# First query block's attention: three score buffers, values of two key tiles a visit, and queries projected with the whole array into one bank

## The chip, the cores and the metric

The kernel runs on one core of one Trainium2 chip. Its engines work from queues of their own and meet through semaphores: TensorE (PE, which multiplies and writes only the eight banks of PSUM; its weight loads are listed apart as PEld), VectorE (DVE), ScalarE (ACT), GpSimd (POOL) and SyncE (SP, which here only starts transfers). Each queue runs in order: an instruction that waits holds up all that stand behind it on its engine. The metric is the device time of one execution in microseconds (us), as the median of several runs; smaller is better.

## The reference

A transformer block on one sequence of 2048 tokens of width 576, in float32: multi-query attention with 32 query heads of 18 and one shared head of keys and values, then a bilinear feed-forward layer of inner width 4608.

```python
def _A_ref(x, wq, wk, wv, wo):
    q = (x @ wq).reshape(B, S, 32, 18).transpose(0, 2, 1, 3)
    k, v = x @ wk, x @ wv
    p = softmax(einsum("bhqd,bkd->bhqk", q, k) * 18 ** -0.5)
    o = einsum("bhqk,bkd->bhqd", p, v)
    return o.transpose(0, 2, 1, 3).reshape(B, S, 576) @ wo

def _B_ref(x, w_gate, w_up, w_down):
    return ((x @ w_gate) * (x @ w_up)) @ w_down

h = x + _A_ref(_layernorm(x), wq, wk, wv, wo)
out = h + _B_ref(_layernorm(h), w_gate, w_up, w_down)
```

## The kernel before

The queries are cut into four blocks of 512 tokens (`TB`), the keys into 16 tiles of 128, the heads into eight groups of four. Attention of one block and one group takes 32 **pairs** (`pair`): a pair multiplies one tile of keys with the queries of two heads (`scores`, L701: two matmuls, each on one half of the array's rows, side by side, into the two banks of a score buffer `s`) and lets ScalarE write the exponentials of that buffer, 128 x 1024, into a tile `P` (L702). Two pairs make the four heads of one key tile; that tile then waits in `pend` until `flush` multiplies it with the values (`values`, L706: eight instructions that work on columns of the array in groups of 32) and adds to the bank `acc`. When all 16 tiles are in, VectorE transposes `acc` into `os` (`turn`, L732) and normalises it (`normalise`, L787 to L794) a round or two later. The eight groups of one block are 256 pairs. Softmax is taken against an upper bound of each score row, which is worked out from sums of absolute queries: `bounds` (L554 on TensorE, then three VectorE operations on a tile `m2`) and `bounds_last` (L543) for the last four heads of all blocks.

Everything is put in order by hand (`manual_schedule`): the order of the calls in the Python program is the order in every queue. The stages are these.

- `keys_values` normalises x, makes keys and values and the first two sevens of block 0's queries, and has done six pairs when it ends.
- The **loop** in `run` (L1600) goes on with the attention of block 0. Beside it run, from a generator `rest`, the remaining fourteen projections of queries (`queries`, seven heads each: 14 steps over the parts of the contraction, L498), and from `down_weights` one step of the work that splits the down weights into a high and a low part (DMA loads by GpSimd, sums L1519 and casts L1527 on GpSimd, subtractions L1533 on VectorE, stores L1539 by SP). A round of the loop is: pair, some steps of a projection (2.3 a round on average, `RATE`; a finished projection counts 4), pair, `run_aux`, values of all but the newest key tile, one step of the weights' work.
- A step of a projection is two matmuls of 64 rows each, side by side on the two halves of the array's rows, into two banks `psq` and `psr` of the tag `f`. At the end VectorE adds the two and splits the sum into a high and a low part `qs` (L505 to L508), SP stores it (L510, L511), and VectorE writes its absolute values `tq` (L515). The tiles `qs`, `m2` and `m2l` share one tag with two buffers, used in turn.
- After the loop, plain rounds (`steps`) go on to the end of group 7 (pair 224), where the bounds are tested (`flag`, `guard`). Group 7's pairs follow, among output projections (L880) that use the banks `f`, and then `ffn`, block by block, with the attention of the later blocks between its matmuls.

PSUM is fully used: two score buffers `s` of two banks (four banks), two banks `f`, one `m`, one `a`. The bank of `acc` is `a` for even and `m` for odd groups of block 0 (`ps_acc`), and `bounds` takes the other one.

Of the kernel before, what the change touches and what calls it, by code (L numbers as in the profile page):

```python
# [18 lines left out]
F32 = mybir.dt.float32  # L19
# [38 lines left out]
class Block:  # L58
# [8 lines left out]


    def ps_s(self, name):
        return self.ps.tile([P, 2, TB], F32, tag="s", bufs=2, name=name)  # L70

    def ps_f(self, name):
        return self.ps.tile([P, TB], F32, tag="f", bufs=2, name=name)

    def ps_m(self, name):
        return self.ps.tile([P, TB], F32, tag="m", bufs=1, name=name)
# [10 lines left out]

    def ps_acc(self, b, g):

        self.in_m = b == 0 and g < 6 and g % 2 == 1  # L90
        return (self.ps_m if self.in_m else self.ps_a)(f"acc{b}_{g}")


    def split(self, hi, lo, src, copy=None):
# [44 lines left out]
    def keys_values(self):  # L139

        pe, act, dve, sp, pool = self.pe, self.act, self.dve, self.sp, self.nc.gpsimd
# [33 lines left out]
        rs, xhs, trs, psks, tq_last = {}, {}, [], {}, []  # L175
# [196 lines left out]
        _, _, tail = trs.pop()  # L372
# [38 lines left out]
        psg = []  # L411
# [43 lines left out]
        psg = bound(kab, self.ps_m("psb1"))  # L455
# [17 lines left out]
    def queries(self, b):  # L473

        pe, act, dve, sp = self.pe, self.act, self.dve, self.sp
        for i, (h0, n) in enumerate(QT):
            r = n * DH
            psq = self.ps_f(f"psq{b}_{i}")
            w_h, w_l = self.wq[i]
            if b == 0 and i < 2:  # L480
                for k, (w, m) in enumerate(passes(w_h, w_l, self.XT[b])):
                    pe.matmul(psq[:r], w, m, start=(k == 0), stop=(k == 13))
                    yield 1
                qs = self.qb.tile([P, 2, TB], F32R, tag="qs", name=f"qs{b}_{i}")
                act.copy(qs[:r, 0], psq[:r])
                if i == 0:
                    yield 0
                    t = f32(self.qb.tile([P, 2, TB], F32R, tag="qs", name="q_f")[:r, 0])
                    act.copy(t, psq[:r])
                    self.nc.gpsimd.tensor_tensor(qs[:r, 1], t, f32(qs[:r, 0]), ALU.subtract)  # L490
                else:
                    dve.tensor_tensor(qs[:r, 1], psq[:r], f32(qs[:r, 0]), ALU.subtract)
            else:

                psr = self.ps_f(f"psr{b}_{i}")
                for k, (w, m) in enumerate(passes(w_h, w_l, self.XT[b])):
                    for o, ps in ((0, psq), (64, psr)):
                        pe.matmul(ps[:r], w[o:o + 64], m[o:o + 64], start=(k == 0), stop=(k == 13))  # L498
# [6 lines left out]
                dve.tensor_copy(t, psr[:r])  # L505
                dve.tensor_tensor(f32(qs[:r, 1]), psq[:r], t, ALU.add)
                dve.tensor_copy(qs[:r, 0], f32(qs[:r, 1]))
                dve.tensor_tensor(qs[:r, 1], f32(qs[:r, 1]), f32(qs[:r, 0]), ALU.subtract)  # L508
            rows = self.q_dram[b, h0 * DH:h0 * DH + r]
            sp.dma_start(rows[:, 0:2, :], f32(qs[:r]))  # L510
            sp.dma_start(rows[:, 2, :], f32(qs[:r, 0]))  # L511
# [6 lines left out]
        if b == NB - 1:  # L518
            yield 4
            self.bounds(b)  # L520

    def bounds(self, b, copy=None, m2=None, psg=None):

        pe, dve, sp = self.pe, self.dve, self.sp
        if psg is None:
            psg = (self.ps_a if self.in_m else self.ps_m)(f"psg{b}_{self.known[b]}")
# [136 lines left out]

    def p_tile(self, shape, name):

        i = self.p_next = (self.p_next + 1) % (P_BUFS + (P2_BUFS if self.p2 is not None else 0))
        pool, tag = (self.pp, "P") if i < P_BUFS else (self.p2, "P2")
        return pool.tile(shape, F32, tag=tag, name=name)

    def more(self, b):  # L670
# [20 lines left out]

    def again_scores(self, n):

        to = [self.ps_f(f"again{i}") for i in range(2)]
        for _ in range(n):
            for i, o in enumerate((0, 64)):
                self.pe.matmul(to[i], self.kT[o:o + 56, 0:P], self.q[o:o + 56, 0], start=True, stop=True)

    def scores(self, s_, p_, q, t, pr):
        for i, o in enumerate((0, 64)):  # L700
# [855 lines left out]
    def run(self):  # L1556
        from contextlib import ExitStack
        tc = self.tc
# [13 lines left out]
        self.tqs, self.in_m = [], False  # L1572
        self.p2, self.p_next, self.wo_from, self.due = None, -1, 10 ** 6, 0.0
        with ExitStack() as st:
            pool = lambda name, bufs, **k: st.enter_context(tc.tile_pool(name=name, bufs=bufs, **k))
            cp, self.lp, self.hp = pool("const", 1), pool("ln", 2), pool("resid", 2)
# [8 lines left out]
            with tc.tile_pool(name="p0q", bufs=1) as self.p0q:  # L1585
                self.wq_in, self.wq = self.wq, {}
                self.XT = [self.p0q.tile([P, 9, TB], F32R, tag=f"XT{b}", name=f"XT{b}") for b in range(NB)]
                self.G = self.p0q.tile([P, 64], F32R, name="G")
                with tc.tile_pool(name="qb", bufs=2) as self.qb:
                    first = self.keys_values()  # L1590
# [230 lines left out]
```

## Time and profile before

| | us |
|---|---|
| median of 3 runs (lowest, highest) | 2250.22 (2249.98, 2252.01) |
| the profiled execution | 2249.05 |
| its span, first to last instruction | 2247.3 |
| TensorE busy in the span | 2222.8 (99%) |
| ScalarE busy | 1434.3 (64%) |
| VectorE busy | 1373.1 (61%) |
| GpSimd busy | 902.6 (40%) |

A line of the profile names an engine, a line of the kernel, an operation, its tiles (out<-in), a count, and microseconds. In a timeline the first number is the start from the beginning of the span, the second how long the group of like instructions lasted; what stands in brackets is idle time of that engine just before, and what ended it. Matmuls overlap, so that the time a matmul takes from the queue is read from start to start, not from its own length.

### The profile page before, as it was taken

Reading aid. Unit: us, or ns where it says so; the run is one execution under the profiler, and the core shown is the slowest. Engines: PE = TensorE matmul, PEld = TensorE weight load, DVE = VectorE, ACT = ScalarE, POOL = GpSimd, SP = SyncE. Lnnn points to the kernel's source line nnn. Section 1 sums busy time; section 2 is a strip of 40 time slices with the busy share of each in tenths; the row PEclk is TensorE's granted clock in tenths of the full one; section 3 lists DMA queues with packets and bytes.
Section 4 is the critical chain, followed back from the end, with each engine's and each line's share of the span. In section 5 each row is a group of like instructions: output and inputs, shape, how many; then the busy total and the mean of one; then the engine's idle time right before and its main releaser. Section 6 shows DMA issues by size and latency. Waiting matters only on the chain.

```text
span 2247.3 us, 45977 instructions
## 1 busy us (share of the span) xinstructions
PE 2222.8 (99%) x17972; PEld 1626.0 (72%) x17972; DVE 1373.1 (61%) x2206; ACT 1434.3 (64%) x1948; POOL 902.6 (40%) x979
## 2 busy tenths in 40 slices
PE   7999999999999999999999999999999999999999
PEld 5333345777777777777777777777777888999999
DVE  8565635565556557455555556545555668888776
ACT  7888877656666666666665666665666534555553
POOL 4444401444344435344444434433332465322222
PEclk9999999999999999999999999999999999999999
DMA  5878843555455565555455554664332445677775
GB/s 176 274 252 291 296 152 96 165 172 169 153 169 166 164 187 160 172 171 175 152 167 163 180 160 160 179 196 148 116 121 96 145 150 200 221 238 239 235 247 174
DMA packets 200625, 407.01 MB, mean 181 GB/s; under 512 B 22573, under 2 KB 54445, under 8 KB 200405
## 3 DMA queue, kind: packets, MB, share of 16 engines
q1 hardware_dynamic: 197813, 393.42, 54.2%
q0 software_dynamic: 2592, 10.62, 1.5%
q8 instruction: 143, 2.34, 0.4%
q14 instruction: 77, 0.63, 0.1%
HBM read 317.27 MB, written 74.55 MB: 174 GB/s over the span
## 4 chain that ended last, share of the span: by engine, by line
PE 83%; DVE 1%; DMA 1%; POOL 1%; ACT 1%; issue 0%; SPq 0%; ACTq 0%; DVEq 0%; POOLq 0%
PE pg L1104 21%; PE acc L706 15%; PE y L1044 13%; PE s L701 9%; PE gs L1330 8%; PE pu L1104 5%; PE yq L1296 4%; PE gu L1104 3%; PE yo L880 3%; PE gs L1337 2%; PE y L1011 1%; DMA h<-in_x_dram 1%; POOL h L1054 0%; PE tx L934 0%; DMA out_dram<-h 0%
## 5 line engine op out<-in xcount | busy, mean ns | idle before, releaser
L702 ACT ACTIVATE P<-s 128x1024 f32<-128x1024 f32 x1024 | 1009.4, 1028 | 214.4 <-PE s L701 131.8
L1104 PE MATMUL pg<-X,ws 64*128 64x512 f32 x2511 | 679.6, 389 | 0.5 <-DVE os L732 0.2
L1104 PE MATMUL pu<-X,ws 64*128 64x512 f32 x2511 | 679.8, 389 | 0.0
L1104 PEld LDWEIGHTS pg<-X,ws 64*128 64x128 f32 x2511 | 465.0, 185 | 77.3 <-issue 2.1
L706 PE MATMUL acc<-P,V 128*32 128x512 f32 x4096 | 479.5, 597 | 0.1
L1104 PEld LDWEIGHTS pu<-X,ws 64*128 64x128 f32 x2511 | 464.5, 185 | 13.5
L701 PE MATMUL s<-q,kT 56*128 56x512 f32 x2048 | 421.3, 414 | 4.8 <-ACT P L702 4.0
L1054 POOL TENSOR_TENSOR h<-h,tmp 128x288 f32<-128x288 f32 x320 | 259.8, 843 | 321.9 <-ACT tmp L1053 320.5
L1053 ACT COPY tmp<-y 128x288 f32<-128x288 f32 x320 | 127.8, 400 | 336.5 <-PE y L1044 307.3
L1044 PEld LDWEIGHTS y<-wdo,room 128*128 128x128 f32 x2142 | 289.7, 188 | 42.4 <-issue 37.7
L701 PEld LDWEIGHTS s<-q,kT 56*128 56x128 f32 x2048 | 194.4, 184 | 172.6 <-ACT P L702 122.7
L1044 PE MATMUL y<-wdo,room 128*128 128x288 f32 x2142 | 303.5, 300 | 1.1 <-DVE room L97 1.0
L706 PEld LDWEIGHTS acc<-P,V 128*32 128x32 f32 x4096 | 114.4, 109 | 254.5 <-issue 250.1
L1050 DVE TENSOR_TENSOR h<-h,y 128x288 f32<-128x288 f32 x394 | 169.5, 453 | 182.5 <-PE y L1044 179.4
L969 DVE TENSOR_TENSOR ws<-wr,ws 128x1152 fp32r<-128x1152 f32 x108 | 189.4, 1754 | 107.3 <-POOL ws L966 107.3
L1142 DVE TENSOR_TENSOR hf<-pu,hf 128x512 f32<-128x512 f32 x93 | 63.8, 686 | 221.5 <-ACT hf L1138 221.5
L966 POOL CAST ws<-wr 128x1152 fp32r<-128x1152 f32 x108 | 131.7, 1220 | 143.0 <-DMA wr<-in_wgu_dram 131.4
L96 POOL CAST room<-hf 128x256 fp32r<-128x256 f32 (+1 forms) x92 | 58.1, 632 | 315.5 <-DVE hf L1142 315.5
L1279 POOL TENSOR_TENSOR wsum<-wsum,wsum 128x512 f32<-128x512 f32 x72 | 145.9, 2026 | 46.4 <-DMA wsum<-in_wgs_dram 39.3
L97 DVE TENSOR_TENSOR room<-hf,room 128x256 fp32r<-128x256 f32 (+1 forms) x108 | 95.4, 883 | 3.4 <-ACT room L96 1.8
L1104 PE MATMUL gu<-X,ws 64*128 64x512 f32 x810 | 94.6, 389 | 0.0
L1104 PEld LDWEIGHTS gu<-X,ws 64*128 64x128 f32 x810 | 78.6, 184 | 13.6 <-issue 1.3
(268 smaller groups left out, 2760.2 us busy)
## 6 DMA issues: line engine op xcount, KB each, us to landing
wdo<-wd_dram SPq DMA_DIRECT2D x492, 288.0 KB
wr<-in_wgu_dram SPq DMA_DIRECT2D x108, 576.0 KB
wsum<-in_wgs_dram SPq DMA_DIRECT2D x108, 256.0 KB
wd_dram<-wd_room SPq DMA_DIRECT2D x20, 1008.0 KB
wsum_dram<-wsum SPq DMA_DIRECT2D x72, 256.0 KB
raw<-wsum_dram SPq DMA_DIRECT2D x72, 256.0 KB
q<-q_dram SPq DMA_DIRECT2D x64, 216.0 KB
raw<-in_wgs_dram SPq DMA_DIRECT2D x54, 256.0 KB
```

The source lines that it names most:

```text
L701: self.pe.matmul(s_[:, i], self.kT[o:o + 56, t * P:(t + 1) * P], q[o:o + 56, pr], start=True, stop=True)
L702: self.act.activation(p_, s_, AF.Exp, scale=SCALE)
L706: self.pe.matmul(acc[32 * j:32 * j + 32, :], self.V[:, t, :], Ps[j // 2][:, j % 2, :], start=first, stop=last, skip_group_check=True)
L966: self.nc.gpsimd.tensor_copy(w[:, 0], self.wr[n])
L969: self.dve.tensor_tensor(w[:, 1], self.wr.pop(n), f32(w[:, 0]), ALU.subtract)
L1044: pe.matmul(y[:, :HD], m[:, t * P:(t + 1) * P], k, start=(first and j == 0), stop=(j == 2), skip_group_check=True)
L1050: dve.tensor_tensor(hs, hs, y[:, :HD], ALU.add)
L1053: act.copy(z, y[:, :HD])
L1054: pool.tensor_tensor(hs, hs, z, ALU.add)
L1104: pe.matmul(ps, w[o:o + 64, wk, c], X[o:o + 64, xk, c], start=(j == 0), stop=(j == 26))
L1279: pool.tensor_tensor(to, x, y, op)
L1330: pe.matmul(bank[:, g * HT:(g + 1) * HT], W[:, wk, c, g], X[:, 2 * xk + c], start=(first and g == c == wk == xk == 0), stop=(c == 1 and wk ...
```

## The change

1. While the two banks `f` aren't needed (from the end of `keys_values` to eight pairs after the guard), they are a third score buffer `s3`, and every third pair uses it. After that the pool `f` is opened again.
2. A new loop, `trio`, takes the place of the old one. A round has four pairs and two steps of the weights' work, and the values of two key tiles in one visit: pair, a run of a projection's steps, pair, pair, pair, values of two tiles.
3. A step of a projection is one matmul over all 128 rows of the array into one bank, `m`. The runs are written out: 5, 5, 4 steps in three rounds for twelve of the projections, 4, 4, 3, 3 for the last two. VectorE makes high and low part with two operations instead of four.
4. `bounds` and `bounds_last` wait in a list `late` and get a round of their own, in place of a run, at the end of a projection. They use the bank `m` too, and `acc` always uses `a`.
5. The exponentials' tiles `P` get four more buffers (`P1`) during the loop. `again_scores`, which keeps TensorE at work at the guard, takes a score buffer instead of two banks `f`.

The diff, without what only renames or makes room:

```diff
     def ps_s(self, name):
+        self.n_s += 1
+        if self.pf is None and self.n_s % 3 == 0:
+            return self.p3.tile([P, 2, TB], F32, tag="s3", bufs=1, name=name)
         return self.ps.tile([P, 2, TB], F32, tag="s", bufs=2, name=name)
...
     def ps_acc(self, b, g):
-        self.in_m = b == 0 and g < 6 and g % 2 == 1
-        return (self.ps_m if self.in_m else self.ps_a)(f"acc{b}_{g}")
+        return self.ps_a(f"acc{b}_{g}")
...
-        self.aux.append((self.round + 1, lambda: self.bounds_last(tq_last), None))
+        self.late.append(lambda: self.bounds_last(tq_last))
...
     def queries(self, b):
...
-                psr = self.ps_f(f"psr{b}_{i}")
+                psq = self.ps_m(f"psq{b}_{i}")
                 for k, (w, m) in enumerate(passes(w_h, w_l, self.XT[b])):
-                    for o, ps in ((0, psq), (64, psr)):
-                        pe.matmul(ps[:r], w[o:o + 64], m[o:o + 64], start=(k == 0), stop=(k == 13))
+                    pe.matmul(psq[:r], w, m, start=(k == 0), stop=(k == 13))
                     if k < 13:
                         yield 1
-                    if self.tqs and self.tqs[0][0] < max(b, 1) and (b and k == 12 or k >= 5 and 4 <= self.n_pair % (2 * NT) < 2 * NT - 6):
-                        self.bounds(self.tqs[0][0])
                 qs = self.qb.tile([P, 2, TB], F32R, tag="qs", name=f"qs{b}_{i}")
-                t = f32(qs[:r, 0])
-                dve.tensor_copy(t, psr[:r])
-                dve.tensor_tensor(f32(qs[:r, 1]), psq[:r], t, ALU.add)
-                dve.tensor_copy(qs[:r, 0], f32(qs[:r, 1]))
-                dve.tensor_tensor(qs[:r, 1], f32(qs[:r, 1]), f32(qs[:r, 0]), ALU.subtract)
+                dve.tensor_copy(qs[:r, 0], psq[:r])
+                dve.tensor_tensor(qs[:r, 1], psq[:r], f32(qs[:r, 0]), ALU.subtract)
...
             self.tqs.append((b, h0, n, tq))
+            if i == 3 or b == 0 and i:
+                self.late.append(lambda: self.bounds(b))
...
+    def trio(self, others, work):
+        self.pair()
+        runs, z = iter(RUNS), 4
+        while z or self.late:
+            self.pair()
+            if self.late and z != 1:
+                self.late.pop(0)()
+            else:
+                for _ in range(next(runs, 1)):
+                    z = next(others, None)
+            self.run_aux(1)
+            next(work, None)
+            self.pair()
+            self.pair()
+            self.pair()
+            self.flush(2)
+            self.run_aux(1)
+            next(work, None)
+        self.pair()
...
     def run(self):
...
                     first = self.keys_values()
+                    two.close()
+                    self.pf = None
+                    self.p3 = two.enter_context(tc.tile_pool(name="s3", bufs=1, space=PSUM))
...
-                    others, live, due = rest(), True, 0.0
-                    while live:
-                        self.pair()
-                        due += RATE
-                        while due > 0 and live:
-                            z = next(others, None)
-                            live = z is not None
-                            due -= z or 0
-                        self.pair()
-                        self.run_aux(1)
-                        self.flush(len(self.pend) - 1)
-                        next(work, None)
+                    with tc.tile_pool(name="P1", bufs=P1_BUFS) as self.p1:
+                        self.trio(rest(), work)
...
             self.steps(lambda: self.n_pair < n + 8)
+            two.close()
+            self.p3, self.pf = None, pool("f", 1, space=PSUM)
...
-RATE = 2.3
+RUNS = (5, 5, 4) * 12 + (4, 4, 3, 3) * 2
+P1_BUFS = 4
```

More of the change, by code (lines that the diff above doesn't have):

```diff
@@ L69, in ps_s @@
     def ps_s(self, name):
+        self.n_s += 1
+        if self.pf is None and self.n_s % 3 == 0:
+            return self.p3.tile([P, 2, TB], F32, tag="s3", bufs=1, name=name)
         return self.ps.tile([P, 2, TB], F32, tag="s", bufs=2, name=name)
     def ps_f(self, name):
-        return self.ps.tile([P, TB], F32, tag="f", bufs=2, name=name)
+        return self.pf.tile([P, TB], F32, tag="f", bufs=2, name=name)
     def ps_m(self, name):
@@ L477, in queries @@
             r = n * DH
-            psq = self.ps_f(f"psq{b}_{i}")
             w_h, w_l = self.wq[i]
             if b == 0 and i < 2:
+                psq = self.ps_f(f"psq{b}_{i}")
                 for k, (w, m) in enumerate(passes(w_h, w_l, self.XT[b])):
@@ L493, in queries @@
             else:
-                psr = self.ps_f(f"psr{b}_{i}")
+                psq = self.ps_m(f"psq{b}_{i}")
                 for k, (w, m) in enumerate(passes(w_h, w_l, self.XT[b])):
-                    for o, ps in ((0, psq), (64, psr)):
-                        pe.matmul(ps[:r], w[o:o + 64], m[o:o + 64], start=(k == 0), stop=(k == 13))
+                    pe.matmul(psq[:r], w, m, start=(k == 0), stop=(k == 13))
                     if k < 13:
                         yield 1
-                    if self.tqs and self.tqs[0][0] < max(b, 1) and (b and k == 12 or k >= 5 and 4 <= self.n_pair % (2 * NT) < 2 * NT - 6):
-                        self.bounds(self.tqs[0][0])
                 qs = self.qb.tile([P, 2, TB], F32R, tag="qs", name=f"qs{b}_{i}")
-                t = f32(qs[:r, 0])
[L505 to L508, printed above, removed]
+                dve.tensor_copy(qs[:r, 0], psq[:r])
+                dve.tensor_tensor(qs[:r, 1], psq[:r], f32(qs[:r, 0]), ALU.subtract)
+                del psq
             rows = self.q_dram[b, h0 * DH:h0 * DH + r]
@@ L516, in queries @@
             self.tqs.append((b, h0, n, tq))
+            if i == 3 or b == 0 and i:
+                self.late.append(lambda: self.bounds(b))
             yield 0 if b == 0 and i < 2 else 4
-        if b == NB - 1:
-            yield 4
-            self.bounds(b)
     def bounds(self, b, copy=None, m2=None, psg=None):
@@ L525, in bounds @@
         if psg is None:
-            psg = (self.ps_a if self.in_m else self.ps_m)(f"psg{b}_{self.known[b]}")
+            psg = self.ps_m(f"psg{b}_{self.known[b]}")
         self.bound_rows(psg, self.tqs)
@@ L664, in p_tile @@
     def p_tile(self, shape, name):
-        i = self.p_next = (self.p_next + 1) % (P_BUFS + (P2_BUFS if self.p2 is not None else 0))
-        pool, tag = (self.pp, "P") if i < P_BUFS else (self.p2, "P2")
+        i = self.p_next = (self.p_next + 1) % (P_BUFS + (P2_BUFS if self.p2 is not None else P1_BUFS if self.p1 is not None else 0))
+        pool, tag = (self.pp, "P") if i < P_BUFS else (self.p1, "P1") if self.p2 is None else (self.p2, "P2")
         return pool.tile(shape, F32, tag=tag, name=name)
@@ L692, in again_scores @@
     def again_scores(self, n):
-        to = [self.ps_f(f"again{i}") for i in range(2)]
+        to = self.ps_s("again")
         for _ in range(n):
             for i, o in enumerate((0, 64)):
-                self.pe.matmul(to[i], self.kT[o:o + 56, 0:P], self.q[o:o + 56, 0], start=True, stop=True)
+                self.pe.matmul(to[:, i], self.kT[o:o + 56, 0:P], self.q[o:o + 56, 0], start=True, stop=True)
     def scores(self, s_, p_, q, t, pr):
@@ L1571, in run @@
         self.n_pair, self.half, self.pend, self.aux, self.round, self.on, self.saving = 0, [], [], [], 0, True, None
-        self.tqs, self.in_m = [], False
-        self.p2, self.p_next, self.wo_from, self.due = None, -1, 10 ** 6, 0.0
+        self.tqs, self.late = [], []
+        self.pf = self.p1 = self.p2 = self.p3 = None
+        self.n_s = 0
+        self.p_next, self.wo_from, self.due = -1, 10 ** 6, 0.0
         with ExitStack() as st:
@@ L1589, in run @@
                 with tc.tile_pool(name="qb", bufs=2) as self.qb:
+                    two = ExitStack()
+                    self.pf = two.enter_context(tc.tile_pool(name="f", bufs=1, space=PSUM))
                     first = self.keys_values()
+                    two.close()
+                    self.pf = None
+                    self.p3 = two.enter_context(tc.tile_pool(name="s3", bufs=1, space=PSUM))
                     work = self.down_weights()
@@ L1598, in run @@
                     self.cast = self.dve.tensor_copy
[L1599 to L1610 removed]
+                    with tc.tile_pool(name="P1", bufs=P1_BUFS) as self.p1:
+                        self.trio(rest(), work)
+                    self.p1 = None
             assert self.n_mx <= 8
```

## The prediction

> **What bounds the kernel now.** I read first the chain of work that ended last, then the loop's stretch alone, from exponential to exponential, then who waits for whom in it, and last TensorE's starts one by one.
>
> ```profile
> PE 83%; DVE 1%; DMA 1%; POOL 1%; ACT 1%; issue 0%; SPq 0%; ACTq 0%; DVEq 0%; POOLq 0%
> ```
>
> TensorE carries the whole span, so what it gains in the first attention ends earlier, if later work isn't held by something else. The loop, by engines (PE, PEld, DVE, ACT, POOL busy, each with its count, then the granted clock, the DMA share and GB/s), and two waits inside it:
>
> ```profile
> 52.69:276.90 224.21, 223.34 (x1632) 85.31 (x1629) 131.17 (x154) 197.77 (x205) 107.73 (x123) 1.00 0.82 275
> ```
>
> ```profile
> ACT P L702 <- PE s L701: 26.4, 89, 1.2
> ...
> PE s L701 <- ACT P L702: 0.8, 4, 0.3
> ```
>
> One of the 205 exponentials began before the stretch and the next after it begins at 277.01 (below), so 204 pairs take 224.3 us, 1.10 each, or 4.40 for four. ScalarE is short of work 89 times (26.4 us); TensorE's matmuls waited for a score buffer 4 times, 0.8 us together. So it is TensorE's own queue that sets the pace. Two rounds of it:
>
> ```profile
> 124.42 1.06 PE L706 MATMUL acc<-P,V 128*32 128x512 f32 x8
> 125.42 0.50 PE L701 MATMUL s<-q,kT 56*128 56x512 f32 x2
> 125.76 0.40 PE L498 MATMUL psq<-XT,wq 64*126 64x512 f32 x1
> ...
> 126.00 0.39 PE L498 MATMUL psq<-XT,wq 64*126 64x512 f32 x1
> ...
> 126.47 0.40 PE L701 MATMUL s<-q,kT 56*128 56x512 f32 x2
> 126.79 1.07 PE L706 MATMUL acc<-P,V 128*32 128x512 f32 x8
> ...
> 128.93 1.07 PE L706 MATMUL acc<-P,V 128*32 128x512 f32 x8
> ```
>
> From start to start: the values of one tile 1.00, the scores behind them 0.34, a step of a projection 0.23 or 0.24 (three of them from 125.76 to 126.47), scores ahead of the values 0.32. A round with three steps is 2.37, with two 2.14. Scores in mid-stream cost 0.23 too (the next fence), so that 0.11 of the 0.34 and 0.09 of the 0.32 are the change between rows in halves and columns in quarters, and the values lose 0.09 at their end.
>
> **The change, part by part.** First a round of `trio` on TensorE, from these starts:
>
> ```profile
> 44.79 1.88 PE L482 MATMUL psq<-XT,wq 128*126 128x512 f32 x7
> 46.60 0.64 PE L706 MATMUL acc<-P,V 128*32 128x512 f32 x4
> ...
> 282.31 0.49 PE L701 MATMUL s<-q,kT 56*128 56x512 f32 x2
> 282.74 1.11 PE L554 MATMUL psg<-tq,G 126*32 126x512 f32 x4
> 283.78 0.50 PE L701 MATMUL s<-q,kT 56*128 56x512 f32 x2
> ...
> 285.20 0.75 PE L701 MATMUL s<-q,kT 56*128 56x512 f32 x4
> 285.88 1.07 PE L706 MATMUL acc<-P,V 128*32 128x512 f32 x8
> ...
> 293.45 1.80 PE L697 MATMUL again<-q,kT 56*128 56x512 f32 x14
> ...
> 428.91 4.05 PE L706 MATMUL acc<-P,V 128*32 128x512 f32 x36
> 432.89 0.67 PE L1044 MATMUL y<-wdo,room 128*128 128x288 f32 x3
> ```
>
> - Values of two tiles: 36 instructions take 3.98 (428.91 to 432.89); less one tile's 1.00, 28 take 2.98, or 0.85 for eight. Two tiles in a visit: 1.85 instead of 2.00.
> - Scores between values and a run: 0.43 (282.31 to 282.74), for they change mode on both sides.
> - A run of five whole-array steps between other modes: seven take 1.81 (44.79 to 46.60), less two at 0.23: 1.35. A step costs no more and no less than one of two halves.
> - Three scores behind the run: two between other modes 0.68 (285.20 to 285.88), the one in the middle 0.23 (six spacings of the seven like pairs at 293.45, (1.80 - 0.40) / 6): 0.91, or 0.89 by the 0.34 and 0.32 above. I take 0.89.
>
> A round with five steps is 1.85 + 0.43 + 1.35 + 0.89 = 4.52, with four 4.29, with three 4.06. The old loop does five steps and four pairs in 2.37 + 2.14 = 4.51. What the double visit saves, the change to the whole array and back eats: a round has four changes of mode, as two old ones had. `RUNS` gives 24 rounds of five, 16 of four, 4 of three; there are seven `late` rounds, four with four bound matmuls (1.04, 282.74 to 283.78; round 4.21) and three with one (3.5 on TensorE, but four exponentials need 3.7, and buffers must come free: 3.8).
>
> The page TensorEngine Tiling of the Trainium skill (Key Properties) says that a change of tiling mode, not of tile, drains the array, which speaks against the runs; the rows agree with about 0.2 a change. Were the whole array free of it, the sum would be that of the second rival below.
>
> **The third buffer** lets TensorE score three pairs in a row. An exponential follows the one before by 0.92 (four in 3.77, the last 1.02 long):
>
> ```profile
> 277.01 3.82 ACT L702 ACTIVATE P<-s 128x1024 f32<-128x1024 f32 x4 [0.20 <-PE s L701]
> ...
> 285.80 3.77 ACT L702 ACTIVATE P<-s 128x1024 f32<-128x1024 f32 x4 [0.39 <-PE s L701]
> ...
> 289.92 1.94 ACT L702 ACTIVATE P<-s 128x1024 f32<-128x1024 f32 x2 [0.35 <-PE s L701]
> ...
> 293.46 1.94 ACT L702 ACTIVATE P<-s 128x1024 f32<-128x1024 f32 x2 [1.60 <-PE s L701]
> ...
> 296.20 3.77 ACT L702 ACTIVATE P<-s 128x1024 f32<-128x1024 f32 x4 [0.80 <-PE s L701]
> 300.21 1.94 ACT L702 ACTIVATE P<-s 128x1024 f32<-128x1024 f32 x2 [0.24 <-ACT P L702]
> ```
>
> Four need 3.7 of a round's 4.5: no wait on TensorE in full rounds, nor a gain there beyond the rounds' own sum. With two buffers only, three scores in a row would wait. The ten `P` tiles cover up to seven live ones.
>
> **The wait at the start.** `m2`, `m2l` and `qs` take turns in two buffers. The old order gave `m2l` a free one and `m2` that of the second projection, still being stored:
>
> ```profile
> 57.31 0.68 DVE L97 TENSOR_TENSOR m2l<-psgl,m2l 32x512 fp32r<-32x512 f32 x1
> ...
> 64.72 0.68 DVE L96 CAST m<-psg 32x512 fp32r<-32x512 f32 x1 [6.14 <-DMA q_dram<-qs]
> 65.44 0.68 DVE L97 TENSOR_TENSOR m<-psg,m 32x512 fp32r<-32x512 f32 x1
> ```
>
> ```profile
> 60.22 0.43 SPq L510 DMA_DIRECT2D q_dram<-qs  x1
> 60.70 0.38 SPq L511 DMA_DIRECT2D q_dram<-qs  x1
> ```
>
> VectorE stood 6.14 us, and TensorE went on, for the bound lay in a bank that it didn't need. In `trio` the first late round takes `m2`, the second `m2l`, and it is `m2l` that gets the buffer under store. SP's queue ahead of that store is as before, so the split of `psgl` again begins at 64.72 and ends at 66.1. But `psgl` is now in bank `m`, and so is the projection that comes in the third round. TensorE would be there at about 61.1 (52.7, where the stretch's first exponential begins, two late rounds of 3.8 and 4.2, 0.43) and stands until 66.1: 5 us, of which nothing comes back, as ScalarE isn't the bound. Behind it stand all scores and values.
>
> **The sum.** From 66.1: the rest of that round 4.09, then 23 x 4.52 + 16 x 4.29 + 4 x 4.06 + 2 x 3.8 + 3 x 4.21 = 209.1, so pair 211 is scored at 279.3. Its exponential begins 0.6 later (285.20 to 285.80). Twelve more by the third buffer, at 0.93, bring pair 223's to 291.1, and as before the last values and pair 224's scores follow, 2.62 after it (290.84, which is 289.92 and 0.92, to 293.46): 293.7 against 293.46. So the loop is some 2 later, and the plain rounds (1.03 a pair before, and the last bounds now inside the loop) give it back. The eight pairs after the guard save 8 x (1.00 - 0.93) = 0.6 (1.00 from 296.20 to 300.21). Together -0.4.
>
> **Other edits.** VectorE per projection, with the two that remain at 0.69 each:
>
> ```profile
> L506 DVE TENSOR_TENSOR qs<-psq,qs 126x512 f32<-126x512 f32 x14 | 9.7, 692 | 0.5
> ...
> L505 DVE COPY qs<-psr 126x512 f32<-126x512 f32 x14 | 9.6, 685 | 27.4 <-PE psr L498 27.3
> ...
> L507 DVE CAST qs<-qs 126x512 fp32r<-126x512 f32 x14 | 8.1, 577 | 0.5
> L508 DVE TENSOR_TENSOR qs<-qs 126x512 fp32r<-126x512 f32 x13 | 12.1, 929 | 0.5
> ```
>
> 2.88 become 1.38: 21 us less of an engine that isn't the bound, worth nothing by itself. The bank is read by both, so it is free 1.4 after the last step. After a run of four the last step ends 1.6 into its round and the bank is wanted at 4.29 + 0.43: slack 1.7. `acc` in one bank must be transposed between two visits:
>
> ```profile
> L732 DVE STREAM_TRANSPOSE os<-acc x7: 703/709/717, 85.7 to 293.0; 128x512 f32<-128x512 f32 x7
> ```
>
> 0.71, with 4.52 - 1.85 = 2.7 between the visits: slack 2.0, six times. Both are hidden as long as VectorE is no later than that. It has waits in the loop that can make it so:
>
> ```profile
> DVE wd_room L1533 <- POOL wd_room L1527: 24.0, 6, 6.2
> DVE wd_src L1533 <- POOL wd_hi L1527: 12.4, 4, 4.8
> ```
>
> Ends: 0 if each falls where VectorE has nothing to hand over, some 10 if five of these ten waits (3.6 on average) stand ahead of a bank's last reader and exceed the slack by 2.0. The weights' work keeps its pace, one step for two pairs, and subtractions mostly stand behind the readers in the order of the calls; I take 0.7. The loads of group 1's queries move a little in SP's queue, behind the same store; they are wanted some twenty pairs later, so nothing. `again_scores` in the third buffer and the reopened `f` (first used by projections a dozen pairs on): nothing, their cover being the exponential two pairs back. Transfers: the same bytes.
>
> So -0.4 + 0.7 = 0.3. The profiled execution (2249.05, of which 1.75 lies around the span) would become 2249.3; the median stands 1.17 above it, which makes 2250.5.
>
> **The rivals.** A measurement of this kernel can tell about 0.2%, 4.5 us, from no change.
>
> 1. No wait at the start: the store lands before 61, or `m2l` gets another buffer. Then 5 us less, 2245.5. For it: only one wait of before shows the late landing. Against: SP issues that store behind the same transfers.
> 2. The change of mode doesn't show around the runs, weights being loaded ahead: a run then costs 5 x 0.23, the scores around it 0.32 and 0.23, in all 0.4 less a round, 44 times: 17 us, 2233. Against: the seven steps at 44.79 take 0.2 more than 7 x 0.23, and the scores at 282.31 the longer 0.43.
> 3. The buffers were the bound, and ScalarE's 26.4 us come back: 2224. Perfetto Trace Analysis of the Trainium skill (Optimization Strategy) reads regular gaps on the engine that should be saturated as possibly too few buffers in PSUM. But the gaps are ScalarE's, and the 0.8 us on TensorE bounds what buffers can give in full rounds.
> 4. Slower: VectorE, held by GpSimd's casts, hands bank `m` or `acc` over late, and TensorE stands, which two spare banks hid before. Decisive from 4 us of such waits in all; with five of ten, as above, 2259.
>
> **How the numbers follow.** My forecast, no change, 0.55; the first rival 0.16; second and third together 0.08; the fourth 0.21. Of the first, half ends beyond 4.5 us. The forecast's own range is 2247 to 2254 (40 full rounds known to 0.05 each, and 0 to 4 for VectorE). All told 2243 to 2258 leaves out the second and third and part of the fourth. Faster 0.18, the same 0.62, slower 0.20.
>
> **What would show it.** Rounds of five at 4.5 with a run of 1.35 and values of 1.85; VectorE's `m2l` waiting for `q_dram` until about 64.7 and TensorE's first `psq` of the loop at 66.1; pair 224's exponential at 293 to 294. Wrong, if the rounds are shorter than 4.4, if that `psq` starts before 63, or if TensorE waits for VectorE at the banks for more than 4 us.

## The result: 0.5% slower, by two long waits of TensorE and the clock after them

| | before | after |
|---|---|---|
| median, us (lowest, highest) | 2250.1 (2249.78, 2252.01) | 2262.59 (2262.21, 2264.65) |
| profiled execution, us | 2249.05 | 2264.65 |
| its span, us | 2247.3 | 2262.9 |
| ratio of the times | | 1.0054, interval 1.0042 to 1.0067 |

In the experiments below, one execution of two (5605.59) and one of plain3 (3615.15) were slow, and no time or ratio given here includes them.

The change costs 12.5 us, outside the range that was given (2243 to 2258). Following single pairs through both traces shows where. The exponential of pair 210 begins 14.9 us later than before, that of pair 224 (where the prediction put 293.7) 13.3 later, that of pair 260 12.6 later; 1.5 is added between pairs 276 and 285, and from pair 300 to the last pair the distance stays at 14.1 to 14.7. So nearly all of it arises in the loop, between 51 and 280 us. ScalarE's timeline of after, at pair 224:

```profile
306.76 1.94 ACT L698 ACTIVATE P<-s 128x1024 f32<-128x1024 f32 x2 [1.66 <-PE s L697]
```

The rounds themselves have the sizes that were predicted. A full round of five steps on TensorE's timeline of after:

```profile
133.08 1.92 PE L702 MATMUL acc<-P,V 128*32 128x512 f32 x16
134.93 0.50 PE L697 MATMUL s<-q,kT 56*128 56x512 f32 x2
135.36 1.43 PE L499 MATMUL psq<-XT,wq 128*126 128x512 f32 x5
136.72 0.96 PE L697 MATMUL s<-q,kT 56*128 56x512 f32 x6
137.61 1.92 PE L702 MATMUL acc<-P,V 128*32 128x512 f32 x16
```

From start to start, values 1.85, scores 0.43, five steps 1.36, three scores 0.89: 4.53. Over the loop the median of the 24 rounds of five is 4.53, of the 16 rounds of four 4.30, of the four rounds of three 4.07 (predicted 4.52, 4.29, 4.06). What is new are two rounds of 11.68 and 10.95 us, and three of 5.26 to 5.48. The waits of TensorE from 51 to 290 us in after (tile and line that waited, what ended it; total, times, longest), without the 0.8 us in all that it waited for score buffers:

```profile
PE psq L499 <- DVE m2l L99: 5.3, 1, 5.3
PE psg L550 <- DVE qs L504: 5.2, 1, 5.2
PE psq L499 <- DVE qs L504: 1.1, 1, 1.1
```

The first is the wait that the prediction had at 5.0. Its place in TensorE's timeline, and the two rows of VectorE that end it:

```profile
61.14 0.50 PE L697 MATMUL s<-q,kT 56*128 56x512 f32 x2
66.98 2.47 PE L499 MATMUL psq<-XT,wq 128*126 128x512 f32 x5 [5.35 <-DVE m2l L99]
69.38 1.65 PE L697 MATMUL s<-q,kT 56*128 56x512 f32 x6
70.96 2.64 PE L702 MATMUL acc<-P,V 128*32 128x512 f32 x16
73.53 0.50 PE L697 MATMUL s<-q,kT 56*128 56x512 f32 x2
```

```profile
65.44 0.68 DVE L98 CAST m2l<-psgl 32x512 fp32r<-32x512 f32 x1 [9.73 <-DMA q_dram<-qs]
66.16 0.68 DVE L99 TENSOR_TENSOR m2l<-psgl,m2l 32x512 fp32r<-32x512 f32 x1
```

`m2l` waits for the store of `qs`, as foreseen. But look at what follows: five steps take 2.40 from start to start where a round at rest has 1.36, three scores 1.58 instead of 0.89, values 2.57 instead of 1.85. The windows around both waits say why. The columns after the busy times (with counts) of PE, PEld, DVE, ACT and POOL are the granted clock, the DMA share and GB/s:

```profile
61.70:65.60 3.90, 0.00 (x0) 0.00 (x0) 0.16 (x1) 1.06 (x2) 3.70 (x5) 1.00 0.77 241
65.70:66.90 1.20, 0.00 (x0) 0.00 (x0) 1.17 (x3) 0.00 (x0) 0.00 (x0) 0.50 0.70 154
66.98:72.40 5.42, 5.42 (x19) 2.69 (x23) 2.68 (x3) 2.16 (x3) 1.58 (x3) 0.50 0.90 315
72.60:77.00 4.40, 4.40 (x33) 1.90 (x29) 0.00 (x0) 2.60 (x4) 3.27 (x4) 1.00 0.71 250
...
157.70:161.10 3.40, 0.00 (x0) 0.00 (x0) 2.94 (x2) 1.02 (x2) 2.03 (x3) 1.00 0.19 47
161.30:162.70 1.40, 0.00 (x0) 0.00 (x0) 1.37 (x4) 0.00 (x0) 0.00 (x0) 0.50 0.66 249
162.77:168.00 5.23, 5.23 (x22) 1.85 (x26) 2.50 (x4) 2.46 (x3) 3.92 (x6) 0.50 0.83 276
```

Some 4 us after TensorE's last matmul the clock goes to half here; it comes back 6.83 us later (72.5 and 168.0), though TensorE is at work again from 66.98 and 162.77. The rest of the round after the first wait lasts 6.55 us (66.98 to 73.53) instead of 4.09: 2.5 us on top of the wait. The second stretch covers 5.23 us of work at half speed, by estimate some 2.6. Before, the clock stands at 1.00 through the whole loop. The Trainium skill, TensorE: Matmul & The Clock Gate (Part 1: The HAM clock gate), has the clock halved after an idle window of some 3.4 us. These two stretches agree, with 4.0 and 3.6 us from the last matmul; other runs below do not (store: 2.0 us after the last matmul; fill and shift: after waits of 2.4 and 1.6 us), and there the measurement decides.

The second wait is a chain over four engines. Its rows on SP, GpSimd, VectorE and TensorE, one timeline each:

```profile
129.57 0.31 SPq L507 DMA_DIRECT2D q_dram<-qs  x1
...
132.66 3.10 SPq L799 DMA_DIRECT2D ob<-ob  x4
135.87 0.58 SPq L1556 DMA_DIRECT2D wd_dram<-wd_hi  x1
136.54 0.61 SPq L1556 DMA_DIRECT2D wd_dram<-wd_src  x1
```

```profile
145.64 0.57 POOL L1530 DMA_DIRECT2D wd_src<-in_wd_dram  x1 [11.16 <-DMA wd_dram<-wd_src]
154.09 3.19 POOL L1536 TENSOR_TENSOR wd_src<-wd_src 128x288 f32<-128x288 f32 x4 [7.87 <-DMA wd_src<-in_wd_dram]
157.22 1.99 POOL L1544 CAST wd_hi<-wd_src 128x864 fp32r<-128x864 f32 x2
```

```profile
126.90 1.32 DVE L1550 TENSOR_TENSOR wd_src<-wd_src,wd_hi 128x1152 f32<-128x1152 f32 x1
...
158.16 3.23 DVE L1550 TENSOR_TENSOR wd_src<-wd_src,wd_hi 128x864 f32<-128x864 f32 x2 [13.96 <-POOL wd_hi L1544]
161.31 0.68 DVE L503 CAST qs<-psq 126x512 fp32r<-126x512 f32 x1
162.02 0.69 DVE L504 TENSOR_TENSOR qs<-psq,qs 126x512 fp32r<-126x512 f32 x1
```

```profile
157.09 0.50 PE L697 MATMUL s<-q,kT 56*128 56x512 f32 x2
162.77 1.91 PE L550 MATMUL psg<-tq,G 126*32 126x512 f32 x4 [5.18 <-DVE qs L504]
```

VectorE had finished the piece of the down weights at 128.2, but its store stands one step of the weights' work later in the program, in SP's queue behind the stores of the queries and of `ob` (which waits for `normalise`). It is issued at 136.5 and has landed at 145.6; only then may GpSimd load the next piece into that tile. Sums and casts follow, and VectorE waits 13.96 us for the cast. Behind that subtraction stand L503 and L504, the only readers of bank `m`, and TensorE needs the bank for `psg`. Reading a wait to its end pays here: the table names `qs`, the cause is a store some 25 us before, as the run store below bears out.

### The profile page after: what moved, and what is told of

Read it like the earlier page. It is cut to its first block, busy times and chain, and to the rows that moved or that the text cites. A ratio compares the mean times of both kernels' runs of the same rounds, so it can differ in the third digit from the quotient of the medians.

```text
span 2262.9 us, 45557 instructions
## 1 busy us (share of the span) xinstructions
PE 2225.7 (98%) x17776; PEld 1635.1 (72%) x17776; DVE 1350.3 (60%) x2181; ACT 1428.2 (63%) x1948; POOL 900.7 (40%) x979
## 4 chain that ended last, share of the span: by engine, by line
PE 89%; DVE 3%; DMA 3%; ACT 1%; POOL 1%; issue 1%; SPq 0%; ACTq 0%; POOLq 0%; DVEq 0%
PE pg L1100 19%; PE acc L702 18%; PE y L1040 13%; PE s L697 11%; PE gs L1326 8%; PE pu L1100 6%; PE yq L1292 4%; PE gu L1100 3%; PE yo L876 3%; PE psq L499 2%; PE gs L1333 2%; DMA wd_dram<-wd_room 1%; ACT P L698 1%; PE y L1007 1%; POOL h L1050 0%
## 5 line engine op out<-in xcount | busy, mean ns | idle before, releaser
L702 PE MATMUL acc<-P,V 128*32 128x512 f32 x4096 | 471.0, 597 | 0.1
L697 PE MATMUL s<-q,kT 56*128 56x512 f32 x2048 | 404.1, 413 | 4.5 <-ACT P L698 3.5
L702 PEld LDWEIGHTS acc<-P,V 128*32 128x32 f32 x4096 | 120.8, 110 | 271.6 <-issue 265.1
```

The costliest lines, as they stand in the source:

```text
L697: self.pe.matmul(s_[:, i], self.kT[o:o + 56, t * P:(t + 1) * P], q[o:o + 56, pr], start=True, stop=True)
L702: self.pe.matmul(acc[32 * j:32 * j + 32, :], self.V[:, t, :], Ps[j // 2][:, j % 2, :], start=first, stop=last, skip_group_check=True)
```

## The experiments

The first theory: the two long waits, each with its stretch of half clock, make the 13 us, and the parts of the round cost what was predicted. Its rivals: the half clock is no consequence of the waits (then shortening TensorE's idle time saves the wait alone); VectorE is late everywhere, so that moving one wait brings up another; and, for the parts that the prediction costed at nothing, that the whole array or the third buffer costs something else than the round's sum.

**The first wait alone (own).** `m2l` in a buffer of its own, one `P1` buffer less for room:

```diff
-        m2 = self.qb.tile([H, 2, TB], F32R, tag="qs", name="m2l")
+        m2 = self.qb.tile([H, 2, TB], F32R, tag="m2l", bufs=1, name="m2l")
-P1_BUFS = 4
+P1_BUFS = 3
```

> m2l has a buffer of its own (for room, three more exponentials' tiles P instead of four). Theory 1, that each of TensorE's two long waits costs its length and then some 2.7 us at half clock: the wait of 5.3 us before the loop's first whole-array step goes, and with it the first stretch at half clock, 8.1 us less than the changed kernel, about 2254.5; the second wait, near 157, stays. Theory 2, that the waits only show a loop held back by the weights' work and its transfers: the time moves to later waits, no less than 2260.

Measured: 2256.76, ratio to the kernel before 1.0032 (1.0020 to 1.0044); 5.8 less than after, where 8.1 were expected. In the profiled execution, the fastest of six (2255.34), the wait and its half clock are gone; at pair 64 the kernel is 1.0 ahead of before where after is 6.7 behind. Pair 224 is 4.0 late. What is left is the second wait, 4.0 us, with a stretch of 3.4 us at half clock. The other executions show lower mean clocks (down to 0.997), and no trace shows where. The long wait, and the window:

```profile
PE psg L550 <- DVE qs L504: 4.0, 1, 4.0
```

```profile
154.70:158.10 3.40, 3.40 (x17) 1.33 (x19) 1.95 (x3) 1.72 (x2) 3.32 (x5) 0.50 0.82 263
```

**The clock alone (fill).** TensorE repeats old scores into a score buffer, 46 matmuls, while it would wait for `m2l`; nothing else is changed:

```diff
-        runs, z = iter(RUNS), 4
+        runs, z, first = iter(RUNS), 4, True
...
+                if first:
+                    first = False
+                    self.again_scores(23)
                 for _ in range(next(runs, 1)):
```

> 23 pairs of score matmuls that nobody reads (5.3 us) stand ahead of the loop's first whole-array step, where TensorE would wait. Theory 1, that an idle TensorE loses its clock: the first step starts at 67.0 as before, but at full clock; 2.7 us less, about 2260. Rival, that the half clock comes from the whole-array runs themselves or from elsewhere: the stretch at half clock stays and the time is the same or a little longer, 2262.6 to 2263.

Measured: 2261.59, ratio 1.0050 (1.0037 to 1.0063), no more than 1.0 less than after, and the intervals overlap. TensorE's timeline and a window of the clock:

```profile
61.71 5.52 PE L693 MATMUL again<-q,kT 56*128 56x512 f32 x46
67.38 1.39 PE L499 MATMUL psq<-XT,wq 128*126 128x512 f32 x5
68.70 0.96 PE L697 MATMUL s<-q,kT 56*128 56x512 f32 x6
```

```profile
66.90:72.40 5.50, 5.35 (x35) 2.43 (x32) 3.16 (x4) 3.13 (x4) 1.21 (x2) 1.00 0.82 288
```

The first step begins 0.4 later than in after, and yet the five steps take 1.32 instead of 2.40: the half clock belongs to the idle time, not to the place. The whole hardly gains, since the later waits stay (4.3 and 2.4 us, with the clock at half from 159.4 and from 272.0): the profiled execution has 1.9 of the gain at pair 64 and has lost it at pair 210. The wait of 2.4 us is much shorter than the two of after and ended at 270.64, and yet there follows:

```profile
272.10:275.40 3.30, 3.30 (x18) 0.93 (x18) 0.35 (x1) 2.65 (x3) 3.20 (x5) 0.50 0.96 322
```

**The second wait alone (store).** The store of a piece goes into SP's queue right behind its second subtraction, not a step later:

```diff
-            for d, f in ((6, lambda p=p: store(p)), (0, lambda p=p: sums(p, 0)), (1, lambda p=p: sums(p, 2)),
-                         (2, lambda p=p: high(p)), (4, lambda p=p: low(p, 0)), (5, lambda p=p: low(p, 1))):
+            for d, f in ((0, lambda p=p: sums(p, 0)), (1, lambda p=p: sums(p, 2)), (2, lambda p=p: high(p)),
+                         (4, lambda p=p: low(p, 0)), (5, lambda p=p: low(p, 1)), (5, lambda p=p: store(p))):
```

> The stores of the weights' work stand in SP's queue right behind the second subtraction, one step earlier, so that they no longer wait behind the queries' stores and the moves of finished heads. Theory 1 (the second wait comes from a late cast of GpSimd, and that from a store that left 7.7 us after its data were ready): GpSimd's loads start some 2 to 7 us earlier, VectorE's 14 us wait for the cast ahead of the fourth projection of block 1 shrinks, TensorE's 5.2 us wait goes with its half clock: about 2254.5, the first wait stays. Theory 2 (the transfers themselves are the limit): the casts come as late as before, 2262.

Measured: 2255.46, ratio 1.0020 (1.0011 to 1.0030). The chain of the second wait, on SP, GpSimd and VectorE:

```profile
127.81 0.52 SPq L1556 DMA_DIRECT2D wd_dram<-wd_src  x1
```

```profile
134.29 0.57 POOL L1530 DMA_DIRECT2D wd_src<-in_wd_dram  x1 [0.74 <-DMA wd_dram<-wd_src]
...
142.34 2.67 POOL L1544 CAST wd_hi<-wd_src 128x864 fp32r<-128x864 f32 x2
```

```profile
154.04 0.69 DVE L503 CAST qs<-psq 126x512 fp32r<-126x512 f32 x1 [6.25 <-PE psq L499]
```

The store is issued 8.7 us earlier, the cast comes 14.9 earlier, and the reader of the bank now waits for TensorE instead of the other way. One line in another queue is worth 7.1 us. The first wait remains, 3.8 us, with its half clock (6.8 us of it, from 2.0 us after the last matmul).

**Both (own_store), and the step of the weights earlier still (own_store4).** The two edits above together; in the second kernel both subtractions and the store stand in one step of the weights' work, at 4 instead of 5.

> The buffer of its own for m2l (three more P tiles instead of four) and the earlier stores together. Theory 1: both long waits and both stretches at half clock are gone, the sum of the rounds alone is left: about 2247, 3 us faster than the kernel before. Theory 2: waits come back elsewhere, 2255 or more.

> As the run before, and the second subtraction moved one step earlier, right behind the first, with the store behind it. Theory 1: GpSimd's loads gain another 2 us or so, and the values of finished groups are turned up to 1.4 us later, which their slack of 2 us covers: 2246 to 2247. Theory 2: 2255 or more.

Measured: 2249.12, ratio 0.9993 (0.9983 to 1.0003), and 2249.18, ratio 0.9995 (0.9985 to 1.0005). TensorE's waits in own_store from 51 to 300 us have no row of VectorE left:

```profile
PE s L697 <- ACT P L698: 2.0, 5, 0.8
PE s L697 <- ACTq L576: 0.4, 1, 0.4
```

Together the two edits take back 13.5 us, all of the 12.5 that the change had cost. So the loss is these two waits with their clock. Without them the kernel cannot be told from the one before: pair 224 is 0.9 and 1.7 ahead of before, and by pair 300 that is nearly gone (0.1 behind and 0.5 ahead), for between pairs 276 and 285 every kernel of these runs but plain3 and the two with repeated scores (0.6 there) loses 1.4 to 1.8 against before, whole with the old loop among them. The cause of that is open.

Both had been expected 2 to 3 us lower. Besides the place just named, the plain rounds keep nothing of their gain: from pair 210 to 224 the two kernels take 16.33 and 16.59 us, and own 16.33, where after and store take 14.90 and 14.91. In own_store one exponential there begins only after ScalarE has stood 1.39 us (at 283.48). What these three kernels share is the `P1` buffer that was given up for room; that it costs the 1.5 us is likely, but no run tests it alone.

**Fill on top of store (fill_store).** Here only the first wait is left, and its idle time is filled.

> The run with the earlier stores, which has only the first wait left, with 23 pairs of score matmuls that nobody reads (5.3 us) ahead of the loop's first whole-array step. Theory 1 (idle time costs TensorE its clock): that step starts at the same time, some 67, but at full clock: 2.7 us less than 2255.5, about 2252.8. Rival (the half clock isn't from idle time): the stretch at half clock stays, 2255.5 or more.

Measured: 2253.27, ratio 1.0010 (1.0001 to 1.0019), 2.2 less than store. The clock stays at 1.00 in the windows from 62 to 280 us, and five steps take 1.35 instead of 2.40. In the two profiled executions the gain does not show (span 2252.7 and 2252.9), since the first step begins at 68.98, where store's stood at 66.46. Of these 2.5 us, 1.5 come from the repeated matmuls, which last longer than the wait did (5.79 from the scores ahead of them to the first step, instead of 4.25). The other 1.0 was there before them: in this execution, the slowest of its eleven, the clock stood at half ahead of the loop, for 6.8 us where store has 3.4 (51.1 to 54.5):

```profile
51.30:58.10 6.80, 6.80 (x32) 2.14 (x28) 3.95 (x7) 5.99 (x7) 3.35 (x3) 0.50 0.56 156
```

So the medians bear the size out, the traces only the mechanism. The traces of own_store, whole and two have such a stretch from 51 us too, for 3.4 us; those of before, after, own and own_store4 have none. No wait of TensorE over 0.42 us stands in the 10 us before it, and its cause is open. With it own_store is 1.0 behind own_store4 at pair 12.

**Moving it the other way (shift).** Subtractions two steps later, store at 8:

```diff
-            for d, f in ((6, lambda p=p: store(p)), (0, ...
-                         (2, ...), (4, lambda p=p: low(p, 0)), (5, lambda p=p: low(p, 1))):
+            for d, f in ((8, lambda p=p: store(p)), (0, ...
+                         (2, ...), (6, lambda p=p: low(p, 0)), (7, lambda p=p: low(p, 1))):
```

> The subtractions of the weights' work are two steps later in the order, and the stores behind them too: the same work on the same engines. Theory 1: the fourth query projection of block 1 is read out before VectorE waits for GpSimd, the bound's split comes behind that wait, TensorE waits about 1 us instead of 5.2 and keeps its clock: about 2256, if no other reader falls behind a wait. Theory 2: 2262 or more, as the weights' work ends two steps later.

Measured: 2266.48, ratio 1.0075 (1.0062 to 1.0088): missed by 10 us, on the wrong side. The `psg` wait is gone, but the later subtractions stand ahead of other readers:

```profile
PE psq L499 <- DVE m2l L99: 5.3, 1, 5.3
PE psq L499 <- DVE m L99: 3.4, 1, 3.4
PE acc L702 <- DVE os L728: 2.1, 2, 1.6
```

Giving GpSimd more time before VectorE comes was the wrong remedy: it delays the store too (138.99 instead of 136.54), and the store is what the next piece waits for (its cast begins at 159.88 instead of 157.22). Besides the stretch after the first wait, the clock is at half from 165.0 to 171.8 and from 243.5 to 246.9, the last after a wait of only 1.6 us, for `acc`.

**The subtraction on GpSimd (gp).** Then VectorE has nothing to wait for:

```diff
-                dve.tensor_tensor(src[:, lo:to], src[:, lo:to], f32(hi[:, lo:to]), ALU.subtract)
+                pool.tensor_tensor(src[:, lo:to], src[:, lo:to], f32(hi[:, lo:to]), ALU.subtract)
```

> The subtractions of the weights' work run on GpSimd instead of VectorE, so that no reader of bank m stands behind a wait for GpSimd's casts. Theory 1: the second wait (5.2 us) and its half clock (2.6 us) go, and the 1.1 us of a late bank elsewhere: about 2253.7; the first wait stays at 5.3. Theory 2: GpSimd needs some 11.7 of 13.2 us for each part of the weights, falls behind, and SP's queue holds up stores and loads of queries: no gain, 2262 or more.

Measured: median 2262.99 (2255.12 to 2267.81), ratio 1.0059 (1.0043 to 1.0074). The profiled execution took 2255.23, with the second wait down to 1.0 and pair 224 4.8 late, as the first theory had it, and another took 2255.12. The other four took 6.8 to 12.6 more, at a mean clock of 0.995 to 0.996 instead of 0.998, and where they lost it no trace shows. Inconclusive.

**The whole array in the old loop (whole).** The kernel before, with nothing but projections over the whole array in one bank and two operations of VectorE instead of four:

```diff
-                    for o, ps in ((0, psq), (64, psr)):
-                        pe.matmul(ps[:r], w[o:o + 64], m[o:o + 64], start=(k == 0), stop=(k == 13))
+                    pe.matmul(psq[:r], w, m, start=(k == 0), stop=(k == 13))
...
-                dve.tensor_copy(t, psr[:r])
-                dve.tensor_tensor(f32(qs[:r, 1]), psq[:r], t, ALU.add)
-                dve.tensor_copy(qs[:r, 0], f32(qs[:r, 1]))
-                dve.tensor_tensor(qs[:r, 1], f32(qs[:r, 1]), f32(qs[:r, 0]), ALU.subtract)
+                dve.tensor_copy(qs[:r, 0], psq[:r])
+                dve.tensor_tensor(qs[:r, 1], psq[:r], f32(qs[:r, 0]), ALU.subtract)
```

> The kernel before with one part of the change: each step of a projection is one matmul over all rows into one bank, and VectorE has two operations instead of four; loop, buffers and order as before. By the starts of the profile a step costs the same 0.23, and a change of mode to the whole array and back 0.42 in each of some 88 rounds that have steps: 37 us slower, about 2287. Rival, that the change of mode is hidden: 2250, or faster by less work on VectorE.

Measured: 2287.21, ratio 1.0151 (1.0130 to 1.0172), 37 us more. A visit of two steps between two scores on TensorE:

```profile
122.37 0.50 PE L696 MATMUL s<-q,kT 56*128 56x512 f32 x2
122.80 0.72 PE L496 MATMUL psq<-XT,wq 128*126 128x512 f32 x2
123.46 0.49 PE L696 MATMUL s<-q,kT 56*128 56x512 f32 x2
123.88 1.06 PE L701 MATMUL acc<-P,V 128*32 128x512 f32 x8
```

Two steps take 0.66 and the scores after them 0.42; a round with two steps has 2.51 in the median where before has 2.13, one with three 2.75 instead of 2.36. So 0.39 a visit for going to the whole array and back, some 34 us by estimate for the 88 visits of the loop; in the profiled execution (2289.45) the distance to before grows by 31.2 between pairs 6 and 210. Another 4.6 of its time is a wait of TensorE at the guard, with 6.8 us at half clock behind it, and whether that belongs to the change of mode no run shows. So that the median meets the expected 2287 is in part luck: the one execution at a mean clock of 1.000 took 2280.71, 31 more than before. This is where the change's promise goes: 44 long visits instead of some 88 short ones, with one visit of the values each, pay the same number of changes in all.

**No third buffer (two).** own_store with the two old score buffers only.

```diff
-        if self.pf is None and self.n_s % 3 == 0:
+        if self.pf is None and self.n_s < 0:
```

> The mended kernel (a buffer for m2l, earlier stores, 2249.1) without the third score buffer. Theory 1 (three scores in a row need it): the fourth score of a round waits for the exponential of the second, 1.1 us in each of 51 rounds, and the plain rounds lose some 2.5 us: about 2308. Rival (the buffers aren't short, as TensorE waited only 0.8 us for them in the kernel before): 2249 to 2252.

Measured: 2317.41, ratio 1.0294 (1.0275 to 1.0313); 2308 was expected. On TensorE the fourth score of a round stands for ScalarE:

```profile
132.33 0.73 PE L697 MATMUL s<-q,kT 56*128 56x512 f32 x4
134.01 0.50 PE L697 MATMUL s<-q,kT 56*128 56x512 f32 x2 [0.94 <-ACT P L698]
```

A round of five takes 5.74 instead of 4.53; 44 times that is 53 of the 68 us between this kernel and own_store, and short stretches of half clock come on top (the one from 64.4 to 67.8 with no wait over 0.95 us before it). Without the third buffer the new order is 3% slower; the buffer's worth is to make it neutral.

**The third buffer in the plain rounds alone (plain3).** The kernel before, with `s3` in use from the end of the loop to eight pairs after the guard.

> The kernel before, its loop untouched, with the third score buffer only from the loop's end to eight pairs after the guard. Plain rounds went from 1.03 to 0.92 us a pair in the changed kernel: about 2 us less, 2247.8. Rival (the end of the stage is set by the loads for the output projections): 2250.

Measured: 2249.16, ratio 0.9994 (0.9984 to 1.0003), pair 256 0.8 ahead of before, where 2 were expected. The sign is as expected, and the size cannot be told from no change.

No version measured beats the kernel before by more than its interval.

## Why the prediction was wrong, point by point

- **The rounds of the new loop** were right to 0.01 each, and with them the step that counted four changes of mode in a round as in two old ones: whole shows the price of the visits, and own_store, with neither wait, is back at the old time. Rivals 2 and 3 (shorter rounds, buffers as the bound) fall: the rounds kept their length, and TensorE waited 0.8 us for score buffers in after too.
- **The wait at the start**, 5.0 us predicted, measured 5.35, from 61.6 to 66.98. That it has nothing to give back was right. Its cost was not: the prediction took it as 5 us of standing still and had no term for the clock, which stays at half for 6.83 us and takes 2.5 more. This is the first failed step, a term that was missing. At the second wait the same missing term comes again: some 2.6 there, 5 in all.
- **VectorE's lateness**, "I take 0.7", measured 5.2 and 1.1. This is the second failed step. The mechanism was rival 4's, at 0.21, but not in its shape: not five waits of some 3.6, each 2.0 over its slack, but one of 13.96 us, 4 times the mean that was used. The quoted rows had the longest at 6.2, taken in a loop whose pace of the weights' work was another; "the weights' work keeps its pace" looked at steps per pair and not at what stands in SP's queue between a subtraction and its store.
- **The sum.** Pair 224 at 293.7 was forecast and 306.76 measured, 13.1 late. The clock after the first wait has 2.5 of this, the second wait 5.2 and its clock 2.6, the third wait 1.1, the first wait's later start and greater length 0.5 and 0.35: 12.2. The remaining 0.9 is not placed.
- **The rest of the sum** was low too. Without its wait it would have been rival 1's 2245.5, and own_store and own_store4, with no long wait, measured 2249.1 and 2249.2. Of that difference some 1.5 probably belongs to the experiment itself (the plain rounds without the fourth `P1` buffer), 0.5 to the loop's first step, at 61.55 in own_store4 instead of 61.1, and 1.6 to 1.8 to pairs 276 to 285, which the prediction took as unchanged; in after they cost 1.5.
- **The plain rounds** gave what was said: from pair 210 to 224 16.45 us before and 14.90 after. The eight pairs after the guard (226 to 234) save 0.73, where 0.6 was said.

A look at the longest single wait, in place of a mean of ten, would have moved the forecast to the slower side with the same profile of before: 6.2 less the slack of 2.0 is 4.2. The price of the clock could not be read from that profile, for there the clock stands at 1.00 through the whole loop.

## What to carry to other kernels

Where TensorE's work stands in line behind another engine's, a wait of some us can cost more than its length: the two of over 5 us here cost 2.5 to 2.6 more each, and waits as short as 1.6 and 2.4 us were followed by half clock as well. So take the cause of such a wait away; a cover of matmuls saves the clock, but not the wait. An in-order queue ties streams together that share no data: when a bank is to be read by an engine that also serves a slow stream, follow that stream back through every queue to the store that frees its buffer, for there a single line was worth 7 us here. And a change that lengthens visits to save changes of mode has to be counted over a whole round: what the values saved here, the projections paid.

## What the hardware showed that was not expected

- The granted clock falls to 0.50 in or after a wait and stays there while TensorE is at work again: in after from 4.0 and 3.6 us after the last matmul, for 6.83 us, 5.4 and 5.2 us of that with TensorE at work; in store from 2.0 us after it, for 6.8 us; in own a wait of 4.0 us was followed by 3.4 us at half.
- These runs give no length of wait from which the clock falls. Stretches of 3.4 us at half followed waits of 2.4 us (fill) and 1.6 us (shift); in five traces one stands at 51 us, with no wait over 0.42 us in the 10 us before it; the wait of 1.1 us in after, at 270.5, was followed by none.
- Matmuls without use keep the clock: with 46 repeated scores in the gap it stayed at 1.00, and the next five steps took 1.32 us instead of 2.40.
- A visit to the whole array costs 0.39 us over the two half-array banks (whole; 31.2 us from pair 6 to pair 210 of the profiled execution).
